# A long-convolution filter and a maxout FFN on one core: positions laid out anew in the prologue

## The chip, the core and the metric

The program runs on one NeuronCore of one Trainium2 chip. Its engines work in parallel, each through its own queue in order: TensorE (PE; its weight loads, PEld, overlap its matmuls), VectorE (DVE), ScalarE (ACT), GpSimd (POOL) and SyncE (SP), which here only issues DMAs. Semaphores order them among each other. The metric is the device time of one execution in microseconds (us), the median of several runs. All data are 32-bit floats.

## The reference

Two blocks follow each other. The first is a convolution over 12,544 positions whose filter comes from a small network and a decay; the second is a maxout feed-forward network.

```python
h_mlp = np.maximum(pos_emb @ w1, 0.0) @ w2        # (12544,64)@(64,64), then @(64,128)
window = np.exp(-0.01 * pos)[:, None]
h_filt = h_mlp * window
u = x * v                                          # batch 4, 12544 x 128
Uf = np.fft.rfft(u, n=2 * S, axis=1)
Hf = np.fft.rfft(h_filt, n=2 * S, axis=0)
y = np.fft.irfft(Uf * Hf[None], n=2 * S, axis=1)[:, :S, :]
x = (x * y).reshape(B * S, D)
h = np.maximum(np.maximum(x @ w1, x @ w2), x @ w3) # 128 -> 768
out = h @ w_out                                    # 768 -> 128
```

## The kernel before

The convolution is done as matrix products. A position is written as n and p: 98 rows n of 128 places p each. A first transform runs over n (90 frequencies), a second over p; the filter's transform is multiplied in, and two inverse steps follow. The filter is cut to 82 rows n, since the decay is zero in 32-bit floats beyond them; they are handled as two halves of 41 rows, one on partitions 0 to 63, one on 64 to 127.

The work has three stages. The **prologue** (to about 110 us) makes the filter before its second product, `hs`, and transforms filter and first batch over n, while the FFN's weights, given as 64-bit floats, are converted on VectorE. Then 45 frequency pairs are carried through for the filter and the first batch (to about 270 us). After that the FFN runs for one batch while the next is transformed. The order of all instructions is written out by hand: what stands first in the program stands first on its engine.

The change touches only the prologue. Its parts, in the kernel's names:

- `pos`, `posv`: the transposed position embedding, loaded as it lies (64 features by 41 x 128 positions, twice) into the first part of the tile `specH`, in four cuts along n (11, 10, 10, 10 rows), each cut by one DMA from ScalarE's queue and one from SyncE's (L315). `posv` is the same memory seen as feature, p, n. For a fixed p the 41 values n lie 128 floats, 512 bytes, apart.
- `mlp_in(i)`, L353: step i of eight. It multiplies for 16 places p the 41 positions of each half by `w1`: 32 matmuls of 64 rows by 41 weights by 64 columns, with the positions as the weights that are loaded into the array. In 32-bit floats one matmul appears in the trace as two pairs of weight load and matmul, so a step is 64 pairs. They go to the four quadrants of the array. Steps alternate between two PSUM banks.
- `mlp_out(i)`, L361: two VectorE instructions that take the step's maximum with 0 and multiply by the decay; they write `hs`.
- The decay: `window_turn` (L330 on TensorE, then four ScalarE copies, L334) and `window_back` (L338 on TensorE, then a copy, L340) turn it into the layout `winr` that `mlp_out` needs. Before, `window_back` stands after the first step.
- `warm_up`, L167: matmuls on zeros while TensorE waits. There are 22 rounds before the decay's turn, and 3 after it, which write into the bank that the turn's copies read.
- Units: the first batch comes in 32 units. They are `u_load`ed by SyncE (L379), multiplied with `v` by VectorE (`u_mul`, L386), turned in pairs on TensorE (`turn2`, L391) and copied by ScalarE (L983), and transformed (`early` and `quad`, both through L176). The buffers of units 0, 2 and 4 are lent to the decay at first, so their loads wait for it.
- After the eight steps sixteen `quad`s (L176 with `f1h`) transform the filter.

The program has one loop over i for the eight steps, in which the turns, transforms and multiplications of the first units stand at fixed places.

Of the kernel before, what the change touches and what calls it, by code (L numbers as in the profile page):

```python
# [16 lines left out]
P = 128  # L17
# [10 lines left out]
HH = NH // 2  # L28
# [67 lines left out]
def kernel(  # L96
# [15 lines left out]
    nc = tc.nc  # L112
# [49 lines left out]
    def halves_mm(out, lhsT, rhs, start, stop):  # L162


        w = block[0]
        for h in range(0, P, w):
            nc.tensor.matmul(out[h:h + w], lhsT[:, h:h + w], rhs,  # L167
                             start=start, stop=stop, skip_group_check=True)
# [58 lines left out]
    def convert(r, i, h):  # L227
# [52 lines left out]
    specH = pin.tile([P, N1, 2, FO], FP32, name="specH")  # L280
    pos = specH[:].rearrange("p k r f -> p (k r f)")[:, 0:HH * P]
    posv = pos.rearrange("f (n p) -> f p n", p=P)
    hs = spec[0:64 + HH].rearrange("p k r d -> p (k r d)")[:, 0:FO * P].rearrange(
        "n (f r t) -> n f r t", r=2, t=64)
    w1_sb = sml.tile([P, FO], FP32, name="w1_sb")
# [26 lines left out]
    cuts = (0, 11, 21, 31, HH)  # L312
# [5 lines left out]
    for r in range(2):  # L318
        nc.scalar.copy(winT[:, r, 0:64], warm[:, 0:64])

    def warm_up(n):

        ps = next(turns_)
        for _ in range(n):
            halves_mm(ps[:, 0:256], warm[:, 0:P], warm[:], True, True)
# [3 lines left out]
    def window_turn():  # L329
        nc.tensor.transpose(pw[:, 0:64 + HH], win, eye[0:64 + HH, 0:64 + HH])  # L330
        for r in range(2):
            for h in range(2):
                c = 64 * (h ^ r)
                nc.scalar.copy(winT[:, r, c:c + HH], pw[:, 64 * h:64 * h + HH])  # L334

    def window_back():
        for r in range(2):
            nc.tensor.matmul(pw[0:64 + HH, 512 + 64 * r:576 + 64 * r], winT[:, r], back[:, r],  # L338
                             start=(r == 0), stop=True, skip_group_check=True)
        nc.scalar.copy(winr[:].rearrange("n r t -> n (r t)"), pw[0:64 + HH, 512:512 + P])  # L340
# [5 lines left out]
    def mlp_in(i):  # L346

        ps = pms[i % 2]
        for q in range(8):
            for r in range(2):  # L350
                for h in range(2):
                    c = 64 * (h ^ r)
                    nc.tensor.matmul(  # L353
                        ps[c:c + HH, 512 * r + q * FO:512 * r + (q + 1) * FO],
                        posv[64 * h:64 * h + 64, P - 1 - 2 * (8 * i + q) - r, :],
                        w1_sb[64 * h:64 * h + 64], start=(q == 0), stop=True,
                        skip_group_check=True)
    def mlp_out(i):
        v = pms[i % 2][0:64 + HH].rearrange("n (r t f) -> n r f t", r=2, t=8)
        for r in range(2):  # L360
            nc.vector.scalar_tensor_tensor(  # L361
                out=hs[:, :, r, 8 * i:8 * i + 8], in0=v[:, r], scalar=0.0,
                in1=winr[:, r, None, 8 * i:8 * i + 8].to_broadcast([64 + HH, FO, 8]),
                op0=ALU.max, op1=ALU.mult)
# [9 lines left out]
    def u_load(b, u):  # L374
        c, g0 = divmod(u if b == 0 else u // 2 + u % 2 * (NU // 2), NG // 4)
        ts = []
        for src in (xr, vr):
            t = pools(b, u).tile([P, 4, NB], FP32, tag=f"u{len(ts)}", name="ut")
            nc.sync.dma_start(  # L379
                t[:], src[4 * g0:4 * g0 + 4, :, c, b, :].rearrange("g p n -> p g n"))  # L380
            ts.append(t)
        us[u] = ts

    def u_mul(u, eng=nc.vector):
        a, v = us[u]
        eng.tensor_tensor(out=a[:], in0=a[:], in1=v[:], op=ALU.mult)  # L386

    def turn(u, ps):
        a, _ = us.pop(u)
        for i in range(4):  # L390
            nc.tensor.transpose(ps[0:NB, i * P:(i + 1) * P], a[:, i, :], eye[:])  # L391
# [442 lines left out]
    def up(i, f, tag="hid", bufs=3):  # L834
        rhs = gs[i][:].rearrange("d p n -> d (p n)")
        h = (hidp if tag == "hid" else lp).tile([P, N], FP32, tag=tag, name="hid", bufs=bufs)
        pa = next(hbanks)
        halves_mm(pa[:, 0:N], w_sb[1][:, f * P:(f + 1) * P], rhs, True, True)
        nc.scalar.activation(h[:], pa[:, 0:N], Relu)  # L839
        pb = next(hbanks)  # L840
        halves_mm(pb[:, 0:N], w_sb[2][:, f * P:(f + 1) * P], rhs, True, True)
        nc.vector.tensor_tensor(out=h[:], in0=h[:], in1=pb[:, 0:N], op=ALU.max)  # L842
        return h
# [133 lines left out]
    def turn2(u):  # L977

        t = utp.tile([NB, 8, 2, 64], FP32, tag="uT", name="uT")
        ps = next(turns_)  # L980
        for v in range(2):
            turn(u + v, ps[:, 512 * v:512 * v + 512])
        nc.scalar.copy(t[:], ps[0:NB, :].rearrange("n (s t r) -> n s r t", s=8, r=2))  # L983
        uts[u] = t

    def quad(lhs, table, *dsts, engines=(nc.scalar.copy, nc.scalar.copy)):
        ps = next(turns_)
        first_halves(ps, lhs, table, dsts, engines)
# [6 lines left out]
    def early(u):  # L995
        t, v = uts[u - u % 2], 4 * (u % 2)
        quad([t[:, v + i] for i in range(4)], (f1, f1), aside[u],
             spec[:, NS:, :, 4 * u:4 * u + 4])

    warm_up(22)  # L1000
    window_turn()
    warm_up(3)
    nc.scalar.dma_start(f1, f1_d)
    for u in range(4):
        u_load(0, u)
# [2 lines left out]
        u_load(0, u)  # L1008
    raws.append(load_raw(*jobs[1], nc.sync))
    for i in range(9):  # L1010
        if i in (4, 7):
            turn2(2 * (i // 7))
            for u in range(6 + 2 * (i // 7), 8 + 2 * (i // 7)):
                u_load(0, u)
        if i in (5, 6):
            early(i - 5)
        if i < 8:
            mlp_in(i)
        if i >= 7:
            early(i - 5)  # L1020
        if i == 0:
            window_back()
            nc.scalar.dma_start(f1h[:], f1h_d)
            nc.scalar.dma_start(w2_in[0:FO], w2[:, :])
            nc.scalar.dma_start(w2_in[FO:P], w2[:, :])
        else:
            mlp_out(i - 1)
        if i in (3, 5):
            for u in range(i - 3, i - 1):
                u_mul(u)  # L1030
    nc.scalar.dma_start(f1e[:], f1e_d)
    for u in (0, 2):
        uts.pop(u)
# [2 lines left out]
    for f in range(0, FO, 4):  # L1036
        quad([hs[:, f + i] for i in range(4)], (f1h[:, 0], f1h[:, 1]), specH[:, :, :, f:f + 4])
        u, k = divmod(f // 4, 4)
# [216 lines left out]
    for n, (b, i) in enumerate(tiles[:LAST]):  # L1255
# [19 lines left out]
        for f in range(NF):  # L1275
# [9 lines left out]
            h = up((b, i), f)  # L1285
# [43 lines left out]
    for i in range(0, NT, 2):  # L1329
        h = {}  # L1330
        X, Y = banks if i % 4 == 0 else banks[::-1]
        for j, (name, f) in enumerate(ORDER):
            n = int(name[1]) - 1
# [66 lines left out]
```

## Time and profile before

| | us |
|---|---|
| median of three runs | 2215.88 (2215.23 to 2217.56) |
| profiled execution: time | 2216.71 |
| profiled execution: span of its core | 2214.9 |
| TensorE busy | 2191.9 (99%) |
| VectorE busy | 1533.7 (69%) |
| ScalarE busy | 1211.1 (55%) |
| GpSimd busy | 1180.0 (53%) |
| first relu-product step starts | 15.86 |
| first transform of the filter starts | 38.4 |
| second stage starts | about 111 |

The page of a profile gives busy times by engine, the span in slices, the DMA queues, the chain of work that ended last, and the costliest groups of instructions. Rows of the trace name engine, source line, the tile written and the tiles read, with the shape. An engine's row in a timeline or chain is start, length, engine, line, count. A line of instructions asked for by its source gives the smallest, median and largest duration in ns. In a table of stretches each row gives the stretch, its length, the busy time of each engine with the number of instructions, the granted TensorE clock (1.00 is full), the share of busy DMA engines and GB/s.

### The profile page before, as it was taken

How to read it: one execution, taken by the hardware profiler on the slowest of the kernel's cores; microseconds unless marked ns; L12 is line 12 of the kernel's file. 1: busy time of each engine (PE TensorE's matmuls, PEld its weight loads, DVE VectorE, ACT ScalarE, POOL GpSimd, SP SyncE). 2: the span in 40 equal slices, each digit the busy share in tenths (PEclk: the TensorE clock that was granted, in tenths of full speed). 3: DMA queues.
4: the chain of work that ended last, by engine and by line, in shares of the span. 5: the costliest groups of instructions: out<-in, count | busy, mean ns of one | idle time of the engine just before them, and what ended most of it. 6: DMA issues, size and time to landing. Idle time of an engine off the chain costs nothing.

```text
span 2214.9 us, 77203 instructions
## 1 busy us (share of the span) xinstructions
PE 2191.9 (99%) x31655; PEld 1295.4 (58%) x31655; DVE 1533.7 (69%) x3293; ACT 1211.1 (55%) x2223; POOL 1180.0 (53%) x1577
## 2 busy tenths in 40 slices
PE   9999899999999999999999999999999999999999
PEld 8988755555555455545555555555555545667776
DVE  5688856668878766667888766668888744454443
ACT  3699845556666555456666555556666622222222
POOL 1166567535545566544444567634454426666665
PEclk9999999999999999999999999999999999999999
DMA  8789999889999899879999999979999632222221
GB/s 199 184 268 316 284 184 189 168 190 245 252 242 243 214 189 174 168 179 245 240 247 240 216 191 185 177 161 248 243 247 243 180 79 59 60 72 70 61 59 24
DMA packets 491332, 411.62 MB, mean 186 GB/s; under 512 B 289406, under 2 KB 407920, under 8 KB 490979
## 3 DMA queue, kind: packets, MB, share of 16 engines
q1 hardware_dynamic: 443689, 274.50, 57.7%
q0 software_dynamic: 45808, 130.25, 21.1%
q8 instruction: 249, 4.08, 0.8%
q10 hardware_dynamic: 1482, 1.93, 0.4%
q14 instruction: 104, 0.85, 0.1%
HBM read 262.85 MB, written 84.67 MB: 157 GB/s over the span
## 4 chain that ended last, share of the span: by engine, by line
PE 91%; DVE 3%; POOL 2%; issue 2%; DMA 1%; ACT 1%; SPq 1%; POOLq 0%; ACTq 0%; DVEq 0%
PE hps L167 46%; PE ops L167 19%; PE ops L903 6%; PE cps L167 4%; PE cps L547 3%; PE cps L449 3%; PE ps L176 3%; PE cps L557 3%; PE ps L167 1%; POOL xt L638 1%; PE last L167 1%; DVE ab L645 1%; DVE xs L637 1%; PE ps L391 1%; POOL specH L638 1%
## 5 line engine op out<-in xcount | busy, mean ns | idle before, releaser
L167 PE MATMUL hps<-gt,w_sb 128*64 128x392 f32 (+1 forms) x7672 | 1158.5, 495 | 0.8 <-DVE gt L829 0.7
L839 ACT ACTIVATE hid<-hps 128x392 f32<-128x392 f32 x768 | 382.7, 498 | 759.0 <-PE hps L167 742.2
L167 PEld LDWEIGHTS hps<-gt,w_sb 128*64 128x64 f32 (+1 forms) x7672 | 430.9, 126 | 440.0 <-issue 408.8
L842 DVE TENSOR_TENSOR hid<-hid,hps 128x392 f32<-128x392 f32 x768 | 428.1, 557 | 346.5 <-PE hps L167 329.3
L167 PE MATMUL ops<-hid,wo_sb 128*64 128x392 f32 x2304 | 476.9, 492 | 0.0
L599 POOL TENSOR_TENSOR cb<-cb,xs 128x512 f32<-128x512 f32 x135 | 177.6, 1316 | 368.3 <-DVE xs L596 345.6
L167 PEld LDWEIGHTS ops<-hid,wo_sb 128*64 128x64 f32 x2304 | 165.7, 137 | 213.6 <-issue 213.6
L572 DVE TENSOR_TENSOR cb<-cps,eo 128x512 f32<-128x512 f32 (+1 forms) x288 | 175.0, 649 | 72.5 <-ACT eo L569 71.5
L857 POOL DMA_DIRECT2D out_dram<-ot x96 | 76.9, 801 | 270.5 <-ACT ot L855 233.6
L587 ACT ACTIVATE xs<-cb 32x512 f32<-32x512 f32 x270 | 169.5, 628 | 21.1 <-DVE cb L572 12.2
L588 ACT COPY xs<-cb 32x512 f32<-32x512 f32 x270 | 166.3, 616 | 3.2
L603 DVE TENSOR_TENSOR xs<-cb 128x256 f32<-128x256 f32 x270 | 148.1, 596 | 7.3 <-POOL cb L599 7.3
L429 ACT COPY uT<-turned 113x512 uint16<-113x512 uint16 x180 | 125.8, 770 | 0.0
L580 POOL DMA_DIRECT2D zd<-cb x135 | 94.0, 697 | 36.1 <-DVE cb L572 35.9
L386 POOL TENSOR_TENSOR ut<-ut 128x392 f32<-128x392 f32 x90 | 92.9, 1033 | 36.4 <-DMA ut<-in_vr_dram 33.3
L167 PEld LDWEIGHTS cps<-f4p,even 90*64 90x64 f32 x1552 | 87.2, 138 | 35.9 <-issue 33.6
L772 POOL DMA_DIRECT2D xT<-in_x_dram x172 | 101.2, 601 | 6.7 <-issue 3.4
L471 DVE TENSOR_TENSOR low<-high,cps 128x180 f32<-128x180 f32 x186 | 54.5, 334 | 67.9 <-ACT high L461 67.9
L928 POOL DMA_DIRECT2D out_dram<-o x120 | 72.6, 610 | 47.0 <-DVE o L921 45.6
L167 PE MATMUL cps<-f4p,zt 90*64 90x49 f32 x1552 | 95.8, 222 | 0.0
L413 POOL COPY planes<-ut 128x392 uint16<-128x392 uint16 x180 | 95.2, 563 | 0.0
L167 PE MATMUL cps<-f4p,even 90*64 90x49 f32 x1552 | 94.6, 220 | 0.0
(172 smaller groups left out, 3335.8 us busy)
## 6 DMA issues: line engine op xcount, KB each, us to landing
ht<-hd SPq DMA_DIRECT2D x264, 256.0 KB, 6.8
wt<-wq_const POOLq DMA_DIRECT2D x144, 256.0 KB, 5.6
zd<-cb POOLq DMA_DIRECT2D x135, 256.0 KB, 5.2
zt<-zd SPq DMA_DIRECT2D x384, 90.0 KB, 4.0
sq<-spec SPq DMA_DIRECT2D x528, 64.0 KB, 5.7
ut<-in_xr_dram SPq DMA_DIRECT2D x128, 196.0 KB, 4.4
ut<-in_vr_dram SPq DMA_DIRECT2D x128, 196.0 KB, 4.5
wt<-wt_const SPq DMA_DIRECT2D x90, 256.0 KB, 5.1
```

The source lines that it names most:

```text
L167: nc.tensor.matmul(out[h:h + w], lhsT[:, h:h + w], rhs, start=start, stop=stop, skip_group_check=True)
L413: nc.gpsimd.tensor_copy(w[:, h, :, :, 0:HB], a[:].bitcast(U16).rearrange("p s (m e h) -> p h s e m", e=2, h=2)[:, h])
L429: nc.scalar.copy(uts[u][0:HR, 8 * (u % 2):8 * (u % 2) + 8].rearrange("n s r t -> n (s r t)").bitcast(U16).rearrange("n (s r t h) -> n h s ...
L572: nc.vector.tensor_tensor(out=cb[:, a, lo:hi], in0=ps[:, lo:hi], in1=eo[:, lo:hi], op=op)
L587: nc.scalar.mul(xs[at:at + 32], xt[at + 32:at + 64], -1.0)
L588: nc.scalar.copy(xs[at + 32:at + 64], xt[at:at + 32])
L599: nc.gpsimd.tensor_tensor(out=xts[g], in0=xts[g], in1=xs[:], op=ALU.add)
L603: nc.vector.tensor_tensor(out=ab[:, q], in0=y[:, 0], in1=y[:, 1], op=(ALU.subtract, ALU.add)[q])
L772: eng.dma_start(xT[c * NG:(c + 1) * NG].rearrange("d i p n -> d (i p) n"), x[:, 4 * i:4 * i + 8, c, b, :])
L839: nc.scalar.activation(h[:], pa[:, 0:N], Relu)
L842: nc.vector.tensor_tensor(out=h[:], in0=h[:], in1=pb[:, 0:N], op=ALU.max)
L903: nc.tensor.matmul(ps[32 * q:32 * q + 32, 0:H2], w[:, m:m + 32], rhs[:, H2 * c:H2 * c + H2], start=start, stop=True, skip_group_check=True)
```

## The change

The positions are copied on chip, cut by cut, into a second region of `specH`, in which for each place p the n values are adjacent (48 floats are set aside for each p, 41 are used). VectorE copies the first two cuts, ScalarE the third. The last cut is copied in eight pieces of 16 places, in the order in which the steps use them, on VectorE, ScalarE and GpSimd. The steps load their weights from the new region.

The decay's `window_back` now stands right after `window_turn`, ahead of the three rounds of warm-up; the pieces of the last cut follow, and after them the load of `f1` on ScalarE's queue. In the loop, the first unit pair is turned ahead of the sixth step instead of the fifth, the first transform stands ahead of the seventh step, the second and third behind the eighth step, and the fourth after the loop; before, two stood ahead of the sixth and seventh step and two behind the eighth. TensorE and SyncE have the same instructions as before; VectorE has five copies more, ScalarE four, GpSimd two.

```diff
+    laid = specH[:].rearrange("p k r f -> p (k r f)")[:, HH * P:HH * P + 48 * P].rearrange(
+        "f (p n) -> f p n", n=48)
...
+    def lay(copy, j, p0, p1):
+        n = slice(cuts[j], cuts[j + 1])
+        copy(laid[:, p0:p1, n], posv[:, p0:p1, n])
+
+    lay(nc.vector.tensor_copy, 0, 0, P)
+    lay(nc.vector.tensor_copy, 1, 0, P)
+    lay(nc.scalar.copy, 2, 0, P)
+
+    def lay_last():
+        copies_ = (nc.vector.tensor_copy, nc.scalar.copy, nc.vector.tensor_copy, nc.scalar.copy,
+                   nc.gpsimd.tensor_copy, nc.gpsimd.tensor_copy, nc.vector.tensor_copy,
+                   nc.scalar.copy)
+        for i, copy in enumerate(copies_):
+            lay(copy, 3, P - 16 * (i + 1), P - 16 * i)
...
-                        posv[64 * h:64 * h + 64, P - 1 - 2 * (8 * i + q) - r, :],
+                        laid[64 * h:64 * h + 64, P - 1 - 2 * (8 * i + q) - r, 0:HH],
...
     warm_up(22)
     window_turn()
+    window_back()
     warm_up(3)
+    lay_last()
     nc.scalar.dma_start(f1, f1_d)
...
     for i in range(9):
-        if i in (4, 7):
-            turn2(2 * (i // 7))
-            for u in range(6 + 2 * (i // 7), 8 + 2 * (i // 7)):
+        if i in (5, 7):
+            turn2(i - 5)
+            for u in range(i + 1, i + 3):
                 u_load(0, u)
-        if i in (5, 6):
-            early(i - 5)
+        if i == 6:
+            early(0)
         if i < 8:
             mlp_in(i)
         if i >= 7:
-            early(i - 5)
+            early(i - 6)
         if i == 0:
-            window_back()
             nc.scalar.dma_start(f1h[:], f1h_d)
...
+    early(3)
```

## The prediction

> **What bounds the kernel now.** I read the page's chain first, then the chain and the timeline of the first 40 us, then single lines. The page's chain:
>
> ```profile
> PE 91%; DVE 3%; POOL 2%; issue 2%; DMA 1%; ACT 1%; SPq 1%; POOLq 0%; ACTq 0%; DVEq 0%
> ```
>
> TensorE carries the end for 91% of the span, and the change lies in its first 40 us. So the question is when TensorE starts on the filter's transforms (L176 with f1h, 38.4 us in the trace): from 38 to 109 us it never rests, and a shift there reaches the end one for one. The chain before that, by time (start, length, what):
>
> ```profile
> 13.52 0.25 PE ps L330
> 14.39 1.52 PE ps L167 x12
> 15.91 1.96 PE ps L353 x58
> 17.87 0.51 PE ps L338 x4
> 18.38 1.68 PE ps L353 x60
> ...
> 24.80 1.68 PE ps L353 x59
> ...
> 34.30 1.68 PE ps L353 x57
> 35.98 3.09 PE ps L176 x75
> ```
>
> The reader sees one engine working almost without a gap: window turn (L330), warm-up (L167), eight relu-product steps (L353), and between them the decay's second turn (L338) and the turns and transforms of units 0 to 3. What held back the first L353 is the positions' landing: SyncE's last of four issues, at 3.6 us, takes 12.3 us, so it is there at 15.9.
>
> ```profile
> L315 SPq DMA_DIRECT2D specH<-in_pos_emb_dram x4: 605/726/847, 1.4 to 3.6; - x4
> DMA to landing us min/median/max: 9.4/10.8/12.3
> ```
>
> What one step costs, over two stretches of one step each, then over one unit's product much later (L449); columns as us, PE busy (x), PEld busy (x), clock, DMA:
>
> ```profile
> 24.73:26.40 1.67, 1.67 (x64) 1.61 (x64) 1.00 0.70 164
> 34.23:35.90 1.67, 1.67 (x64) 1.61 (x64) 1.00 0.83 186
> ```
> ```profile
> 401.93:403.35 1.42, 1.42 (x64) 1.30 (x64) 1.00 0.85 209
> ```
>
> Both place 64 pairs of weight load and matmul in four quadrants. L353 streams only 64 columns under 41 weights and takes 1.67 us (26 ns a pair); L449 streams 90 under 64 weights and takes 1.42 us (22 ns). Its loads are what is slow:
>
> ```profile
> L353 PEld LDWEIGHTS ps<-w_sb,specH x512: 142/197/207, 15.9 to 35.6; 64*41 64x41 f32 x171
> ```
> ```profile
> L449 PEld LDWEIGHTS cps<-f1e,uT x2976: 129/133/137, 284.4 to 1439.6; 49*64 49x64 f32 x199
> ```
>
> Median 197 ns for 41 weights that lie 512 bytes apart, against 133 for 64 adjacent ones.
>
> **The change, part by part.** All against the profiled execution: span 2214.9, its own time 2216.71, which is 0.83 over the median of the three runs, 2215.88.
>
> *The steps' loads become adjacent.* A step of 64 pairs takes 1.67 to 1.75 us, say 1.70. Upper end after: 22 ns a pair as L449, 1.42 us. Lower end: L1135 (128 columns, four quadrants) takes 1.03 us for 32 records, 32 ns; from 32 and 22 ns at 128 and 90 columns a line leads to 15 or 16 ns at 64, 1.02 us. I take the middle, 1.22, as neither end is nearer in weights and columns both: 8 x (1.70 - 1.22) = **-3.8 us** (-5.4 to -2.2). VectorE limits it: a relu product (L361) takes 2 x 0.645 = 1.29 us and frees the bank that the step after next writes. With steps of 1.22 VectorE is slower where no turn or transform lies between, in the first four: **+0.2**. At 1.02 it takes back about 0.9, so the lower end is -4.5.
>
> *The decay's second turn leaves the steps.* L338 takes 0.51 us between the first two (17.87 to 18.38): **-0.5**. It goes ahead of the three warm-up rounds, and there it is in the way, next.
>
> *New copies, and a wait.* VectorE lays out the first two cuts (1408 and 1280 elements), ScalarE the third (1280), and the last comes in eight pieces of 160 on three engines. ScalarE works in order, and the third cut's copy stands **ahead of the four copies of the turned decay** (L334); behind those wait L338, the warm-up (L167, already released by L334 today) and the first step, all in TensorE's order. The third cut lands between SyncE's second (2.28 + 9.4 = 11.7) and fourth (15.9), at about 14.1. The copy's price isn't in the trace. Lower bound: 1024 elements from PSUM in 1.01 and 256 in 0.37 give 0.83 ns each and 0.16 fixed, 1.2 us. The nearest row is ScalarE's one copy that reads SBUF with gaps (16 bytes):
>
> ```profile
> L343 ACT COPY w2x<-w_in x1: 446/446/446, 39.4 to 39.4; 128x128 f32<-128x128 f32 x1
> ```
>
> 0.446 us for 128; 64 adjacent ones take 0.242 and 512 take 0.617 (L319, L588), so 128 adjacent would take 0.30. The gap adds 1.2 ns to 0.84: 0.19 + 1280 x 2.0 = 2.8 us, which I take; upper bound twice that, 5.6. Then 14.1 + 2.8 = 16.9; four copies 0.5; L338 0.5; warm-up 1.5: the first step starts at 19.4 instead of 15.9, **+3.5** (+1.9 to +6.3). The Trainium skill, "SBUF — State Buffer", section "Door 1: The DMA port swizzle", says that an access which leaves its 16-byte line pays a penalty; it gives no price, and it speaks for a slow strided copy as much as for a slow strided load.
>
> VectorE's share is hidden: at 0.93 ns an element (L251, 384 in 0.356) or 2.0, the second cut (landed 11.7) is laid by 14.3, the first piece of the last cut by 16.3, before 19.4. Without that cover (ScalarE fast, start 17.8) it is still early. ScalarE's three pieces (up to 0.5 each) follow the decay's last copy (18.4) and end by 19.9, the first of them before the second step, at 20.6. GpSimd's two are needed by the fifth and sixth steps; at 0.53 for 256 (L1048) they are ready at 17, and its queue holds nothing else until 41.1.
>
> *The clock.* TensorE idles from 13.8 to about 17.5. The trace shows what that does:
>
> ```profile
> 266.00:269.30 3.30, 1.52 (x28) 1.17 (x32) 3.27 (x9) 2.71 (x4) 0.75 (x2) 1.00 0.47 153
> 269.30:272.80 3.50, 3.50 (x55) 2.84 (x50) 3.46 (x8) 2.42 (x5) 1.16 (x3) 0.51 0.77 206
> ```
>
> After 3.3 us with TensorE 46% busy the granted clock is 0.51 for the next 3.5. Here it would double the 1.3 us of warm-up streaming and part of a step. The stretch's phase is unknown: 0 to +1.7, I take **+0.6**.
>
> *Moved in time, same work.* Unit pair 0 is turned ahead of the sixth step, not the fifth; each transform (L176) comes later. ScalarE's copy of the turned pair (L983, 1.05) has the sixth step (1.22) as cover; if that fell to 1.02 the stall is 0.1. On ScalarE's queue the loads of f1, f1h and w2 now stand behind the laying pieces: f1 goes out at about 20 instead of 13.95; first use of f1 is near 29, of f1h near 38. Loads of the fourth unit share DMA semaphores with them and slip from 19.4 to about 23.5; landing after 6.1 us (its row) is 29.6, about when VectorE multiplies that unit. The unit loads on SyncE that waited for L338 (18.46 today) wait for it still, until 17.9. Taken at 0, up to +0.7.
>
> Sum: -3.8 + 0.2 - 0.5 + 3.5 + 0.6 = **0.0**. Profiled time 2216.7, median 2215.9.
>
> **The rivals.**
> *Cheap copy.* ScalarE reads 512-byte gaps at the pace of adjacent data. For: the 720-element evictions (L185) read PSUM 1 KB apart at 0.76 us, no slower. Against: L343. Start at 17.8 (+1.9), idle under 2.5 us, clock stays: -3.8 + 0.2 - 0.5 + 1.9 = -2.2, 2213.7; with steps of 1.02 and their VectorE limit -3.1, 2212.8.
> *Nothing gained on TensorE* (the change doesn't do what it says): pairs are paced by something else than the load and stay at 26 ns. For: L353 never shows it faster, with any neighbour. Against: L449 at 22 ns with more weights and columns. Then +3.5 - 0.5 + 0.6 = +3.6: 2219.5. The Trainium skill, "TensorE: Matmul & The Clock Gate", section "Wait — 56ns, not 53.3ns?", states that start to start never falls below about 25 ns; by that a step takes 1.60 and the sum, as an estimate, is 2.8, 2218.7. This trace disagrees, with 22 ns in L449.
> *The third cut's copy decides, slower.* ScalarE needs 5.6 us or more for it and everything behind it in ScalarE's queue waits: start 22.2, +6.3, clock +1.7: -3.8 + 0.2 - 0.5 + 6.3 + 1.7 = +3.9, 2219.8; from 6.2 us on (4.7 ns an element) it passes +4.43. For: no row has gaps of 512 bytes on ScalarE, and the weight load pays 64 ns more for 41. Against: 16-byte gaps cost 2.0 ns.
>
> **How the numbers follow.** Forecast 0.45, cheap copy 0.25, nothing gained 0.17, slow copy 0.13. A 0.2% step is 4.43 us, about what a measurement of this kernel can tell from no change; the runs before spread by 2.3. No case's centre reaches it, the cheap copy's tail 0.07 of its side, the slow copy and the tail of "nothing gained" 0.12 together: faster 0.07, same 0.81, slower 0.12. Range: from the cheap copy with the fastest steps (2212.8) to just under "nothing gained" and the slow copy, 2219.5.
>
> **What would show it.** The step's pairs: 64 in about 1.2 us, loads near 130 ns (right), or 1.6 and more. ScalarE's laying copy of 1280 elements: 2.8 us. First step at 19.4; TensorE idle before the decay's second turn; clock below 1.00 between 15 and 23 us. First f1h transform near 38.4. A wait of VectorE for the fourth unit's load would be the moved queue's price. I'd be wrong if the positions landed elsewhere in time, or if a shift of 2 us changed the long overlap after 109 us.

## The result, and the profile after

| | before | after |
|---|---|---|
| median, us | 2216.60 (2214.65 to 2218.12, 22 runs) | 2221.19 (2218.09 to 2228.75, 22 runs) |
| profiled execution, us | 2216.71 | 2219.16 |
| its span, us | 2214.9 | 2217.4 |
| first relu-product step starts | 15.86 | 21.73 |
| first transform of the filter (f1h) | 38.44 | 41.5 |
| second stage starts | 110.56 | 113.80 |

The changed kernel is slower: ratio 1.0020, 95% interval 1.0014 to 1.0026, which is 4.6 us. The profiled execution of after lies near the low end of its runs, so the trace shows only +2.45 of the 4.6. The trace gives the order of the loss: 5.9 us later at the first step, 2.8 regained by the filter's first transform, 3.2 late at the second stage, 2.5 at the end.

The page's chain of after, with the share of each engine:

```profile
PE 89%; DVE 3%; POOL 2%; issue 2%; DMA 2%; ACT 1%; SPq 0%; POOLq 0%; ACTq 0%; DVEq 0%
```

TensorE gave up two points of 91, and "DMA" rose from 1% to 2%. The chain of the changed kernel from 12 to 42 us says where (start, length, what):

```profile
2.93 11.84 DMA specH<-in_pos_emb_dram
...
14.89 2.23 issue
17.13 0.49 ACT winT L351 x4
...
17.66 0.98 PE ps L355 x4
...
25.60 0.98 PE ps L370 x52
26.58 0.64 issue
...
30.34 1.12 issue
...
35.67 0.16 issue
...
39.71 0.67 issue
```

Before, this chain was TensorE from 13.5 us on. After, it starts in the third cut's landing (14.8), goes through ScalarE's laying copy (L325; the 2.23 us of "issue" are that copy running) and the four decay copies (L351) to the decay's second turn (L355). The second half is the unexpected one: TensorE stops four times for 0.16 to 1.12 us **in the middle of** a step or of a transform, with no releaser at all. The timeline shows the start in more detail (in brackets the idle time before, and what ended it); these are rows of ScalarE and of TensorE:

```profile
14.85 2.38 ACT L325 COPY specH<-specH 128x1280 f32<-128x1280 f32 x1 [8.72 <-DMA specH<-in_pos_emb_dram]
...
17.66 0.97 PE L355 MATMUL ps<-back,winT 128*105 128x64 f32 x4 [4.85 <-ACT winT L351]
18.98 2.82 PE L167 MATMUL ps<-warm 128*64 128x256 f32 x12 [0.35 <-ACT winr L357]
21.73 2.00 PE L370 MATMUL ps<-w_sb,specH 64*41 64x64 f32 x128
```

And the table of stretches, 3.4 us each, with TensorE's busy time first and the granted clock third from the right:

```profile
13.60:17.00 3.40, 0.00 (x0) 0.00 (x0) 1.21 (x4) 2.15 (x1) 0.80 (x2) 0.68 1.14 264
17.00:20.40 3.40, 2.38 (x12) 1.64 (x14) 0.41 (x1) 1.98 (x9) 0.26 (x1) 0.50 0.45 94
20.40:23.80 3.40, 3.33 (x136) 2.24 (x132) 0.83 (x2) 0.00 (x0) 0.00 (x0) 0.81 0.97 240
```

TensorE waits 4.85 us for the decay copies. In that gap its clock falls to half and stays there over the second turn (0.98 us in the chain instead of 0.51), the three warm-up rounds (2.82 instead of 1.52) and up to the first step. Between these two the warm-up also waits 0.35 us for ScalarE's copy of `winr` (L357), which reads the bank that the warm-up writes.

The steps themselves did get faster. Their weight loads in after:

```profile
L370 PEld LDWEIGHTS ps<-w_sb,specH x512: 110/114/115, 21.7 to 36.7; 64*41 64x41 f32 x171
```

114 ns against 197; and the first two steps, 128 pairs, take 2.00 us (the row at 21.73), 1.00 a step or 15.6 ns a pair, against 1.70. Eight steps at that pace would save 5.6 us. The filter's transforms come no earlier for it: the late first step takes more than that away, and the stops with no releaser take back a part.

### The profile page after: what moved, and what is told of

It reads as the page before. It is cut to its first block, busy times and chain, and to the rows that moved or that the text cites. A ratio compares the mean times of both kernels' runs of the same rounds, so it can differ in the third digit from the quotient of the medians.

```text
span 2217.4 us, 77221 instructions
## 1 busy us (share of the span) xinstructions
PE 2188.4 (99%) x31655; PEld 1283.1 (58%) x31655; DVE 1538.8 (69%) x3298; ACT 1214.0 (55%) x2227; POOL 1180.6 (53%) x1579
## 3 DMA queue, kind: packets, MB, share of 16 engines
q8 instruction: 249, 4.08, 0.8%
## 4 chain that ended last, share of the span: by engine, by line
PE 89%; DVE 3%; POOL 2%; issue 2%; DMA 2%; ACT 1%; SPq 0%; POOLq 0%; ACTq 0%; DVEq 0%
PE hps L167 45%; PE ops L167 19%; PE ops L920 6%; PE cps L167 4%; PE cps L564 3%; PE cps L466 3%; PE ps L176 3%; PE cps L574 3%; POOL xt L655 1%; PE last L167 1%; DVE ab L662 1%; PE ps L408 1%; POOL specH L655 1%; DVE xs L654 1%; PE ps L167 1%
## 5 line engine op out<-in xcount | busy, mean ns | idle before, releaser
L167 PEld LDWEIGHTS hps<-gt,w_sb 128*64 128x64 f32 (+1 forms) x7672 | 426.3, 126 | 443.3 <-issue 410.2
L167 PEld LDWEIGHTS cps<-f4p,even 90*64 90x64 f32 x1552 | 87.2, 138 | 35.9 <-issue 33.2
```

The costliest lines, as they stand in the source:

```text
L167: nc.tensor.matmul(out[h:h + w], lhsT[:, h:h + w], rhs, start=start, stop=stop, skip_group_check=True)
```

## What stops TensorE: its instructions

The page of after has a row for the instruction queue q8, and the page of steps_thrice_after (below), in which TensorE has 1024 pairs more, has the same row:

```profile
q8 instruction: 249, 4.08, 0.8%
```
```profile
q8 instruction: 257, 4.21, 0.8%
```

249 packets for 4.08 MB are 16,384 bytes each. TensorE's 31,655 matmuls and 31,655 weight loads are 63,310 instructions; over 249 packets that is 254 a packet, and 1024 pairs more, 2048 instructions, add exactly 8 packets: 256 instructions a packet, 64 bytes each. So q8 carries TensorE's own instructions, one packet for each 127 or 128 pairs (254 instructions are 127 pairs; what fills the rest of a packet the count does not tell).

The stops in after are apart by as much: counted in the timeline's pairs from the first one of the program they stand behind pair 349, 476, 603 and 731, each 127 or 128 after the one before. The stops without a releaser in the other versions' steps stand behind the same counts, give or take two (347 to 349, 475 to 477, 603 or 604, 731 to 733), whichever instructions lie there. And q8 delivers just ahead of each restart. In the DMA view of after, the stretches 24 to 26, 28.8 to 30, 33.2 to 34.5 and 37.3 to 39 us hold one packet each (packets, MB, share of 16 engines' time), and 26 to 28.5, 30.2 to 33 and 35 to 37 hold none:

```profile
q8 instruction: 1, 0.02, 4.7%
q8 instruction: 1, 0.02, 4.8%
q8 instruction: 1, 0.02, 5.2%
q8 instruction: 1, 0.02, 5.6%
```

4.7% of 16 engines over 2 us is 1.5 us for one packet. The packets come 4.1 to 4.7 us apart; TensorE restarts at 27.22, 31.46, 35.83 and 40.38, about 1.5 us behind the end of each. From a restart to the start of the next packet it is again 1.5 to 1.8 us. 128 pairs that run in 2.00 us use up in half the time what the queue brings in 4.2. Before, 128 pairs took 3.4 us and the turns and transforms between them, with fewer instructions for their time, made up the rest. Its chain has two of the same stops, behind pair 348 and 603, which the prediction passed over with "almost without a gap":

```profile
23.10 0.11 issue
...
32.18 0.36 issue
```

The Trainium skill, "Runtime: NRT & Kernel Launch", section "Instruction fetch mechanics", says that an engine's instructions are refilled in blocks of 16 KiB, 256 instructions, that the next block is fetched while the current one runs, and that the cost of crossing a block's end is mostly hidden. The packet size and the 256 agree with this trace; that it is hidden does not, with 0.16 to 1.12 us of stop per block here.

## The experiments

Two theories, and how far each reaches, were to be told apart. **The queue:** the third cut's copy on ScalarE stands ahead of the decay's copies and delays the first step, with the clock behind it. **The fetch** (F in the expectations): TensorE cannot run these pairs faster than its instructions arrive, so the adjacent loads gain nothing. The rival to F is that the stops come from something the layout brings with it (a bank, a copy, a semaphore) and that the steps gain their 3.8 us once they start on time. A third theory, R in the expectations, is that the later loads of f1 and of the units make the loss. Times of a version are compared with the kernel before on the same chip.

**third_cut_dve.** The change, with the third cut laid by VectorE.

```diff
-    lay(nc.scalar.copy, 2, 0, P)
+    lay(nc.vector.tensor_copy, 2, 0, P)
```

> The changed kernel with one word changed: VectorE, not ScalarE, copies the third cut, so nothing stands ahead of the decay's four copies on ScalarE. Theory Q (the third cut's copy in ScalarE's queue holds up the decay, the warm-up and the first step, and the idle time halves the clock): the decay's copies end before 14.5 us, the first step starts at about 17 instead of 21.7, no half clock before 25 us, and the median falls by 4 to 5 us below the changed kernel, about 1 us below the kernel before. Theory F in addition (from the second step on, TensorE's pace is set by the fetch of its own instructions, about 4.3 us for each 128 pairs): the first f1h transform comes at about 36.8 us, 19.8 after the first step. Without F, at 1.03 us a step and 1.29 us a relu product, it comes at about 34. Rival theory R (the loss comes from the later f1 and unit loads): start earlier, but the median stays within 1.5 us of the changed kernel.

Measured: 2214.26 (2212.83 to 2216.38), before 2214.92, ratio 0.9999 (0.9990 to 1.0008). The first step starts at 16.33, the filter's transforms at 37.91, and the clock stays full until 24 us. The chain of this version:

```profile
16.33 0.44 PE ps L370 x17
...
20.27 0.98 PE ps L370 x52
21.25 1.80 issue
...
24.37 1.79 PE ps L408 x8
26.16 2.06 PE ps L370 x63
...
```

This one line takes away the whole loss, although the loads of f1 and of the units stand where the change has them, so R falls. The queue is shown: where a copy of 2.4 us stands in ScalarE's order costs 4.6 to 5.3 us of the program (the change's +4.6 against this version's -0.7, or the distance of their ratios, 0.0021, which is 4.7). But the steps that now start in time, with loads of 114 ns, bring nothing against before that these runs can tell: they stop for 1.80 us after the 52nd pair of a step, the program's pair 349. I had expected the filter's transforms at 36.8 with F and at 34 without it; at 37.91 they came later than either.

**moves_only.** The change without the layout: the second turn and the units stand where the change puts them, the steps read the positions as they landed.

```diff
-    lay(nc.vector.tensor_copy, 0, 0, P)
-    lay(nc.vector.tensor_copy, 1, 0, P)
-    lay(nc.scalar.copy, 2, 0, P)
...
-                        laid[64 * h:64 * h + 64, P - 1 - 2 * (8 * i + q) - r, 0:HH],
+                        posv[64 * h:64 * h + 64, P - 1 - 2 * (8 * i + q) - r, :],
...
-    lay_last()
```

> The change without the new layout: the steps load their weights 512 bytes apart as before, but the decay's second turn stands ahead of the warm-up and the first units are turned a step later. Theory Q: the decay's copies end at about 14.3, the first step starts at about 16.3, the steps take 1.70 us, the first f1h transform comes at 38.0 to 38.5, and the median is within 1 us of the kernel before. If the moves themselves cost: 2 us or more above the kernel before.

Measured: 2214.94 (2212.49 to 2218.27), before 2214.92, ratio 1.0001 (0.9992 to 1.0010); first step 15.95, transforms of the filter 36.88. The moves cost nothing that can be told from an interval of 2 us to either side. The transforms came 1.1 us earlier than I had expected (38.0 to 38.5) and 1.5 earlier than in the trace of before, and the median does not show it.

Beside third_cut_dve this is the direct test of the layout, in the same order. From first step to first filter transform moves_only takes 20.93 us with loads of 196 ns, third_cut_dve 21.58 with loads of 114, in one traced execution of each. That stretch, in moves_only and then in third_cut_dve:

```profile
15.95:36.88 20.93, 20.59 (x655) 19.56 (x657) 14.62 (x27) 4.61 (x8) 0.00 (x0) 1.00 0.95 229
```
```profile
16.33:37.91 21.58, 18.24 (x656) 16.08 (x658) 16.39 (x33) 5.35 (x11) 0.78 (x2) 0.92 0.87 212
```

And what TensorE waited for there (us in total, times, longest):

```profile
PE ps L366 <- issue: 0.6, 2, 0.3
```
```profile
PE ps L370 <- issue: 2.0, 2, 1.8
PE ps L176 <- issue: 0.9, 1, 0.9
PE ps L370 <- DVE specH L325: 0.8, 1, 0.8
PE ps L370 <- DVE spec L378: 0.3, 1, 0.3
```

With the layout TensorE works 2.35 us less (18.24 instead of 20.59) and stands idle 3.0 us more (3.34 instead of 0.34). Of the idle time 2.9 us are stops without a releaser, the rest is VectorE's relu products (L378); the 0.8 us for the laying piece (L325) is the wait ahead of the first step and lies outside the stretch, as do 0.2 of the 0.6 in moves_only. At 8 x (1.67 - 1.00) the pairs alone would have saved 5.4 us of work. The clock, which fell to 0.59 of full in the stretch from 23.8 to 27.2 us, behind the stop of 1.80, took 1.8 of that (the unit turn L408 1.79 us instead of 1.01, the step behind it 2.06 instead of 1.03); the other 1.2 I did not take apart. The two medians, of 11 runs each, differ by 0.7 us the other way. So the layout brings nothing that can be measured, on a start in time.

**steps_thrice_after and steps_thrice_before.** The changed kernel and the kernel before, each with every step's matmuls issued three times (the same values are computed again; nothing is left out).

```diff
-        for q in range(8):
+        for _ in range(3):
+            for q in range(8):
...
```

> The changed kernel with each step's 32 matmuls issued three times over (same values), 1024 pairs more. Theory F: from the second step on 128 pairs take 4.2 to 4.5 us, with TensorE idle in each 128 for about half of it and no engine or DMA of the kernel named for it; the eight threefold steps and what lies between take about 50 us. Without F (the loads' or the array's pace, 16 ns a pair): about 2 us for 128 pairs, 25 us for the eight and some 7 us for what lies between.

> The kernel before with each step's 32 matmuls issued three times over, weights 512 bytes apart. Theory F (instruction fetch, about 4.15 us for 128 pairs under this load, whatever the pairs cost below that): TensorE idles about 0.7 us at each 128 pairs, and from the first step to the first f1h transform it takes about 54 us, within 2 us of the changed kernel's threefold steps (54.2), although its loads take 197 ns and the other's 114. If the loads set the pace: 24 x 1.70 + 7.9 = 48.7 us here, and the threefold steps after must be limited by something of their own.

Measured, in one execution of each: from first step to first filter transform, 54.2 us in the changed kernel (19.84 to 74.06; whole time 2251.43) and 50.4 in the one before (15.90 to 66.31; 2243.91). A part of the chain of steps_thrice_after:

```profile
25.97 2.00 PE ps L371 x122
27.97 3.38 issue
...
38.41 2.00 PE ps L371 x128
40.41 1.73 issue
```

and of steps_thrice_before:

```profile
25.74 0.99 issue
26.73 3.07 PE ps L354 x107
29.80 0.66 issue
30.46 3.06 PE ps L354 x110
33.51 1.50 issue
...
38.08 0.39 issue
```

Both run one block of 128 pairs, then stop (the chain counts fewer pairs in some blocks; the timeline has 128, and the lengths tell: 2.00 us and 3.07). Where nothing lies between the steps, a block with quick loads takes 2.00 us and the stop behind it 1.6 to 3.4; with slow loads 3.07 and 0.4 to 1.5. With the pairs in threefold number, loads of 114 ns are not quicker than loads of 195 ns. That rules out the rival to F: stops of the same spacing come without any layout, in the code of before, as soon as turns and transforms no longer thin out the steps.

I had expected the two within 2 us; they are 3.8 apart, the quick one slower. The 50.4 us lie nearer to the 48.7 that I gave for a pace set by the loads, but that figure had no stops in it, and stops are 4.1 us of the 50.4 and 17.3 of the 54.2. In the changed kernel the clock, too, fell behind three of the longer stops (at 31.5, 55.4 and 69.0 us); the 256 pairs from 31.35 took 5.47 us instead of 4.00. The rest of that I did not measure apart.

Another rival is that the packets are late because other transfers crowd the DMA engines, which were full in three of the four stretches above. The same trace has stretches without any: in its DMA view from 38.4 to 46.2 us two packets stand in all, both of instructions, and TensorE stops for 1.73 and 2.09 us all the same.

```profile
DMA packets 2, 0.03 MB, mean 4 GB/s; under 512 B 0, under 2 KB 0, under 8 KB 0
q8 instruction: 2, 0.03, 1.7%
```

**dve_fine_warm and moves_fine_warm.** third_cut_dve and moves_only, with the 22 warm-up rounds of 256 columns ahead of the decay's turn replaced by 56 rounds of 96, which have 136 pairs more (`next(turns_)` keeps the order of the banks).

```diff
-    warm_up(22)
+    for _ in range(56):
+        halves_mm(acc[1][:, 0:96], warm[:, 0:P], warm[:, 0:96], True, True)
+    next(turns_)
```

> The kernel with the third cut on VectorE; the 22 first rounds of warm-up (256 columns) become 56 rounds of 96 columns: about the same time, 136 pairs more. Nothing else moves, but the place in the instruction stream at which TensorE stands when the positions have landed does. Theory F: the stretch of 128 pairs after the one in work is fetched before the first step, the stall of about 1.8 us in the third and fourth steps goes, and the first f1h transform comes 1 to 2.5 us earlier than 37.9 at a first step near 16.3; the median falls by 1 to 2 us. Without F: first step, f1h transform and median unchanged within 0.5 us.

> The moves without the new layout, with the same finer warm-up. Theory F: pairs of 26 ns take 3.4 us for 128, so that only 0.6 us of stalls was left to lose: first f1h transform at 36.3 to 36.9, median 0 to 1 us below the moves alone (2214.9 there).

Measured: 2219.4 (2216.93 to 2223.54), ratio 1.0017 (1.0008 to 1.0026), and 2218.58 (2217.61 to 2221.31), ratio 1.0016 (1.0007 to 1.0025); before 2215.21. Both miss what I expected, with F and without it: I had taken it that a block more would be fetched while TensorE waits for the positions. The chain of dve_fine_warm:

```profile
7.96 5.44 PE ps L167 x131
13.40 1.66 issue
...
15.30 0.29 PE ps L347
```

A stop stands now in the warm-up itself, behind pair 223, in a stream of matmuls on zeros that wait for nobody: 1.66 us here, 1.75 in moves_fine_warm. That is one block ahead of 349, a place that without the finer warm-up lies in the steps, where third_cut_dve stops for 0.17 us. The decay's turn starts 3.1 us later than in third_cut_dve and 2.2 later than in moves_only, the stop and in the first a longer warm-up together. The clock then falls (0.51 from 17.1 to 20.5 us in dve_fine_warm), and the first step starts at 19.9 and 19.5. More instructions on TensorE, in a place where it had nothing to do, cost 3.4 to 4.2 us, with and without the layout.

**laid_only.** The layout as in the change, everything else in the order of before.

```diff
     window_turn()
-    window_back()
     warm_up(3)
     lay_last()
...
         if i == 0:
+            window_back()
...
```

> The new layout without the moves: copies as in the change (third cut on ScalarE, ahead of the decay's copies), but the decay's second turn behind the first step and the first units turned where they were. Theory Q: ScalarE still holds up the decay's copies until 17.6 us and the warm-up that writes the same bank, the first step starts at 19 to 20.5 us, and the median lies 3 to 5 us above the kernel before. If the loss needs the moves: within 1.5 us of the kernel before.

Measured: 2217.62 (2216.16 to 2220.47), ratio 1.0011 (1.0002 to 1.0020), before 2215.21: +2.4 us, where I had expected 3 to 5. Its chain:

```profile
16.48 2.74 PE ps L167 x12
19.22 1.43 PE ps L370 x64
20.65 0.53 PE ps L355 x4
```

The layout alone loses about half by the medians, though the intervals overlap. That the other half needs the layout **and** the early second turn is argued, not shown: in the change L355 runs at half clock, too, and the warm-up waits behind it for ScalarE's copy of `winr`; here the warm-up starts as soon as the decay's copies have ended, and the second turn runs at full clock behind the first step. But here the third cut was also there at 13.65 us, 1.2 earlier than in the trace of the change, and the units' moves are taken back together with the turn. The order without the layout (moves_only) costs nothing that can be told.

**warm_kept and clock_kept.** The change, with more matmuls on zeros between the decay's two turns, so that TensorE does not idle; warm_kept adds 44 pairs, clock_kept keeps the number of pairs by making them wider (a round of `wide_up` has 512 columns).

```diff
     window_turn()
+    for _ in range(11):
+        halves_mm(acc[1][:, 0:256], warm[:, 0:P], warm[:], True, True)
     window_back()
```

```diff
-    warm_up(22)
...
+    warm_up(11)
+    wide_up(6)
     window_turn()
+    wide_up(5)
     window_back()
```

> The changed kernel with 11 rounds of warm-up more, on the other bank, between the decay's turn and its second turn, so that TensorE works while ScalarE copies the third cut. The queue's delay stays, the half clock goes. Theory Q: no half clock between 13 and 25 us, the second turn still at 17.7, the first step at about 19.8 instead of 21.7, the median about 2 us below the changed kernel and its spread smaller. If the clock costs nothing: first step and median as in the changed kernel.

> The changed kernel with TensorE kept at work while ScalarE copies the third cut, and with as many warm-up pairs ahead of the first step as the changed kernel has, so that the places of the fetch stalls stay: 11 rounds of 256 columns and 6 of 512 at first, 5 of 512 between the decay's turn and its second turn. Theory Q with the clock: no half clock between 13 and 24 us; second turn still at 17.5 to 18, first step 2.2 us behind it, at 19.7 to 20.3 (4.1 behind it and 21.7 in the changed kernel); the first f1h transform 1.3 to 2 us earlier than 41.5, and the median about 1.5 us nearer to the kernel before, so 2.5 to 3.5 us above it. If the half clock costs nothing because the fetch sets the pace anyway: first step earlier, f1h transform and median as in the changed kernel, 4.6 above.

Measured: 2219.35 (2218.05 to 2220.70), ratio 1.0022 (1.0012 to 1.0031), before 2214.92; and 2220.01 (2218.27 to 2221.70), ratio 1.0020 (1.0010 to 1.0029), before 2215.41. In both the clock is 1.00 from 13.6 to 27 us, and the way from the start of the second turn to the first step falls from 4.1 us to 2.3 and 2.4. Yet the time is that of the change. The filling ends late (second turn at 18.9 and 18.4 instead of 17.7), so the first step comes only 0.5 and 0.9 us earlier, and the stops of the fetch take that and more. The chain of clock_kept:

```profile
25.66 1.62 issue
...
30.40 3.04 issue
```

Two stops of 4.7 us together, and the filter's transforms begin at 43.7, 2.2 us later than in the trace of the change. Nor was the clock kept for good: it falls behind these stops instead (0.50 from 33.6 to 37.0 us in clock_kept, and from 27.6 to 31.0 in warm_kept). And the traces compare unlike executions: that of clock_kept, 2221.66, is among its slowest, that of the change, 2219.16, among its quickest. What the fallen clock alone costs in the median is therefore not shown; that these two fillings do not recover it is.

## Why the prediction was wrong

I forecast 2215.9 (2212.8 to 2219.5), no change. It was 2221.2, slower. By its own steps:

- **"8 x (1.70 - 1.22) = -3.8"** failed in its mechanism. About TensorE's own pace I was too careful: 15.6 ns a pair, at the quick end of my two rows. But the step assumed that pairs can be issued as fast as they are executed. They come in blocks of 128 every 4 us or so, and the kernel before was near that already. On a start in time and in the same order (third_cut_dve beside moves_only) the layout is worth +0.65 us by the traces and -0.7 by the medians, nothing clear of the spread, where I had -3.8. In the trace of the change the stretch from first step to the filter's transforms is 2.8 us shorter than before (19.8 against 22.6), where -3.8, +0.2 and -0.5 make -4.1: TensorE's work fell by 5.6 us (16.44 against 22.07), but its idle time rose from 0.48 to 3.35, stops of 2.6 and the waits for VectorE.
- **"+3.5" for the third cut's copy and "+0.6" for the clock**: the mechanism was right, step by step (copy ahead of L351, L355, warm-up, first step), the size was not: 21.73 instead of 19.4, or 20.0 with the clock's term. In the trace this is the larger miss: 1.8 us of the 3.1 by which the filter's transforms came late, against 1.3 in the steps. The copy itself was 2.38 us, less than the 2.8 that I took, and until the decay's copies began 2.28 had gone: -0.5. The cut landed at 14.85, not 14.1: +0.75. Half clock over L355 and the warm-up: 0.47 + 1.25 = 1.7, the upper end of my own range, on top of a first step that I had put at 19.4 without any. And 0.35 for the copy of `winr`, which I had not seen to stand between second turn and warm-up. Together 2.3. The size is not fixed, though: steps_thrice_after, the same program up to there, had the third cut at 13.70, its second turn at full clock and its first step at 19.84.
- **"+0.2" for VectorE** as the limit: TensorE waits 0.8 us for L378, near the 0.9 that I gave for the fastest steps, and four times the term.
- **"-0.5" for the decay's second turn** and **"0" for the moved units and loads** are not contradicted: moves_only is 2214.94 beside 2214.92, and its interval of 2 us to either side can't tell 0.5 from nothing.
- The rivals. "Nothing gained on TensorE" (2219.5) came out in its effect where the steps started in time, but by a mechanism that I had not on my list; its own ground, pairs that stay at 26 ns, is wrong. By the Trainium skill's floor of 25 ns start to start ("TensorE: Matmul & The Clock Gate", section "Wait — 56ns, not 53.3ns?") steps would take 1.60 us, as an estimate; this trace has 15.6 ns a pair in four quadrants, and disagrees. "Cheap copy" (1.2 us) and "slow copy" (5.6 and more) are both out, at 2.38; that the slow copy's 2219.8 lies nearest to the measured 2221.2 is luck.

What would have shown it beforehand: the two stops of 0.11 and 0.36 us in the chain of before, inside steps, with no releaser, and the row of q8, whose packet count divides TensorE's instructions by 254.

What stays open: why the change's runs spread over 10.7 us where those of before spread over 3.5; how much of the 4.6 us is the clock; and what sets the 4 us of a fetch (a packet takes 0.9 to 1.5 us of it, about 1.5 pass before TensorE runs on, and 1.5 to 1.8 more before the next packet starts, as if it were asked for only when the block ahead of it has begun; no run takes this apart). To the spread belongs that the third cut was there between 13.65 and 14.85 us in the traces in which ScalarE copies it, and everything behind it moves along. None of the versions is clearly quicker than before; the best, third_cut_dve, is 0.7 us under it, within its interval.

## What to carry to other kernels

An engine that runs many short instructions can be limited by their delivery: multiply the instructions by 64 bytes, find the instruction queue's row, and compare how long a packet's worth of them runs with how far its packets are apart before pricing a faster load or matmul. A stop in the middle of a loop, at "issue" with no releaser, that comes back at the queue's count of instructions points to that limit, and here filler work of many small instructions made it worse. And a copy put on a helper engine is priced by what stands behind it in that engine's order: 2.4 us on ScalarE cost 5.9 at TensorE's first step in the trace of the change, with the clock lost in the wait, and 3.9 in steps_thrice_after beside steps_thrice_before. Last, one trace is one execution: differences of 1 to 2 us between two traces are judged by the medians.

## What was not expected of the hardware

- TensorE's instructions reach it in packets of 16,384 bytes, 256 instructions, 3.3 to 5.6 us apart in the threefold steps, and it restarts 1.2 to 1.7 us behind a packet's end, with the DMA engines full or empty. Pairs of matmul and load at 15.6 and at 24 ns are then not sustained: 128 in 2.00 us and 1.6 to 3.4 us of nothing, or 128 in 3.07 us and 0.4 to 1.5.
- Pairs of 41 adjacent weights by 64 columns run at 15.6 ns in four quadrants. Weights 512 bytes apart load in 197 ns, adjacent ones in 114.
- A copy that reads 32-bit floats 512 bytes apart takes 2.38 us for 1280 on ScalarE (1.9 ns each) and 1.62 on VectorE (1.3 ns); pieces of 160 take 0.47 on ScalarE and 0.55 on GpSimd.
